# Two warm-up matmuls fewer, and two transposed copies exchanged between ScalarE and VectorE, in the opening of a linear-attention and SwiGLU kernel

## The chip, the cores and the metric

One core of a Trainium2 chip. The metric is the device time of one execution in microseconds (us). Executions of one kernel differ by some tenths of a microsecond, so medians are given with their spread. A profile is one execution. Its span runs about 1.8 us shorter than the time of the execution. Engines are named as in the profile: PE (tensor engine, matmuls), ACT (ScalarE), DVE (VectorE), POOL (GpSimd), SP (SyncE, which issues loads and stores).

## The reference, cut to what matters

Inputs q, k, v are 8 batches x 8 heads x 576 tokens x 64, in float32. Attention without a score matrix comes first, a gated feed-forward block after it.

```python
q_s = softmax(q, over the 64 features)
k_s = softmax(k, over the 576 tokens)
kv  = einsum('bhsd,bhse->bhde', k_s, v)        # one 64x64 matrix per head
x   = einsum('bhsd,bhde->bhse', q_s, kv)       # then to tokens x 512
g   = x @ w_gate
out = (g * sigmoid(g) * (x @ w_val)) @ w_out   # 512 -> 1536 -> 512
```

## The kernel before: the parts that matter

Heads are worked in two groups of four per batch (G = 0, 1). The opening is batch 0's attention, written out by hand: it has to end before the first gate matmul. `BANKS` splits the nine token blocks into five and four, one PSUM bank each. `spin(n)` issues n matmuls on zeros, only to keep PE busy.

```python
for G in range(NG):                       # loads of batch 0, on SyncE
    load("q", q, 0, G); kd.append(load("k", k, 0, G))
d = nc.gpsimd.dma_start(out=v16[0], ...)  # values, cast on the way, after the first keys
for t0, t1 in BANKS:                      # values of group 1, in two pieces
    nc.gpsimd.dma_start(out=v16[1][:, :, 64*t0:64*t1], ...)
... # then the weights w_gate / w_val in slices, then w_out in four slices (w_dma), on GpSimd

spin(8)
spin(6, first)                # the first of them waits for the first row sum
key_sum(0)                    # column sums of exp(k): 9 small matmuls, reciprocal on DVE
turn_pe(0, 0, 0); turn_pe(0, 0, 1)        # PE transposes of the normalised queries
turn_out(0, 0, 0, nc.scalar)              # copy out of PSUM
exp_of("k", 0, 1)
turn_out(0, 0, 1, nc.scalar)
norm_mul(0, 1, BANKS)         # DVE: exp(q) times 1/rowsum, group 1
spin(6)
kv_first(0)                   # first K^T V, 36 matmuls of 64x64
key_sum(1)
scale_first(0, nc.scalar)     # K^T V scaled into kn
turn_pe(0, 1, 0); turn_pe(0, 1, 1)
turn_out(0, 1, 0, nc.vector); turn_out(0, 1, 1, nc.vector)
xp0 = x_mm(0, 0, 0), x_mm(0, 0, 1)
kv_first(1, *BANKS[0]); kv_first(1, *BANKS[1])
... # copies of x, second scaling, x of group 1, copies of x

after = w_dma[0]              # batch 1's loads wait for the first slice of w_out
for what, src in (("q", q), ("v", v), ("k", k)):
    ...load(what, src, 1, G, ..., after=after)
for m in range(MT):           # gate and value matmuls of batch 0's 576 tokens
    m_unit(0, S, m, by_group=(m == 0))
exp_of("q", 1, 0); exp_of("q", 1, 1)      # behind the last silu on ACT
norm_sum(1, 0); norm_mul(1, 0); norm_sum(1, 1)
... # output matmuls of batch 0, between them batch 1's attention:
i = norm_mul(1, 1)
...
turn_pe(1, 1, 0); turn_pe(1, 1, 1)        # the transposes at 46 us
... # then K^T V and x of batch 1, then seven chunks of the feed-forward block
```

The softmax here doesn't subtract the row's maximum and nothing guards it: scores larger than these inputs give would overflow.

Of the kernel before, what the change touches and what calls it, by code (L numbers as in the profile page):

```python
# [15 lines left out]
def kernel(  # L16
# [10 lines left out]
    nc = tc.nc  # L27
# [19 lines left out]
    def bank(name):  # L47
        return psp.tile([128, 512], FP32, tag="ps", name=name)
# [57 lines left out]
    def copy(eng, out, in_):  # L106
        if eng is nc.scalar:
            nc.scalar.copy(out=out, in_=in_)  # L108
        else:
            eng.tensor_copy(out=out, in_=in_)  # L110
# [5 lines left out]
    def exp_of(what, b, G, pieces=((0, T),)):  # L116
        s = st.setdefault((b, G), {})
        e = s["e" + what] = at.tile([128, T, 2, 64], BF16, tag="e" + what, name="e" + what)
        src = raw[what, b, G].rearrange("p h (t d) -> p t h d", d=64)
        for t0, t1 in pieces:  # L120
            nc.scalar.activation(out=e[:, t0:t1], in_=src[:, t0:t1], func=AF.Exp)  # L121
# [21 lines left out]
    def norm_mul(b, G, pieces=((0, T),), engs=None):  # L143
        s = st[b, G]
        eq2 = s["eq"].rearrange("p t h d -> p (t h) d")
        qs = s["qs"] = at.tile([128, T, 128], BF16, tag="qs", name="qs")
        for (t0, t1), eng in zip(pieces, engs or (nc.vector, nc.vector)):
            n = 2 * (t1 - t0)
            last = eng.tensor_mul(  # L149
                qs[:, t0:t1, :].rearrange("p t (h d) -> p (t h) d", d=64),  # L150
                eq2[:, 2 * t0:2 * t1, :],
                s["rr"][:, 2 * t0:2 * t1].to_broadcast([128, n, 64]),
            )
        return last

    def turn_pe(b, G, i):
        s = st[b, G]
        if i == 0:
            s["qt"] = at.tile([128, T, 128], BF16, tag="qt", name="qt")
        t0, t1 = BANKS[i]  # L160
        tp = s["tp", i] = psp.tile([128, 1024], BF16, tag="ps", name="tp")
        for t in range(t0, t1):
            j = t - t0
            nc.tensor.transpose(  # L164
                out=tp[:, j * 128:(j + 1) * 128], in_=s["qs"][:, t, :], identity=ident
            )

    def turn_out(b, G, i, eng):
        s = st[b, G]
        t0, t1 = BANKS[i]  # L170
        copy(
            eng,
            s["qt"][:, t0:t1, :],
            s["tp", i][:, 0:(t1 - t0) * 128].rearrange("p (t c) -> p t c", c=128),
        )
# [19 lines left out]
    def x_mm(b, G, i):  # L195
        s = st[b, G]
        t0, t1 = BANKS[i]
        xp = [bank("xp") for _ in range(2)]
        for g in range(2):
            for h in range(2):  # L200
                r = slice(64 * h, 64 * h + 64)
                nc.tensor.matmul(  # L202
                    out=xp[h][64 * g:64 * g + 64, 0:64 * (t1 - t0)],
                    lhsT=s["kn"][r, g, :],
                    rhs=s["qt"][r, t0:t1, 64 * g:64 * g + 64],
                    start=True, stop=True,
                )
        return xp

    def x_out(b, G, i, xp, engs=(nc.scalar, nc.vector)):  # L210
        t0, t1 = BANKS[i]
        n = 64 * (t1 - t0)
        c0 = b * S + 64 * t0
        for h in (h for h in range(2) if engs[h] is not None):
            copy(engs[h], xt[:, 2 * G + h, c0:c0 + n], xp[h][:, 0:n])
# [137 lines left out]
    with tc.manual_schedule():  # L353
# [31 lines left out]
        def spin(n, after=None):  # L385
            idle = bank("idle")
            for _ in range(n):
                i = nc.tensor.matmul(out=idle, lhsT=zero[:, 0:128], rhs=zero, start=True, stop=True)  # L388
                if after is not None:
                    tc.add_manual_dep(i.ins, after.ins.name, SYNC, reason="start of the warm-up")  # L390
                    after = None
# [12 lines left out]
        def kv_first(G, t0=0, t1=T):  # L404
            s = st[0, G]
            if t0 == 0:
                s["kv"] = [bank("kv") for _ in range(2)]
            for t in range(t0, t1):
                for g in range(2):
                    for h in range(2):  # L410
                        nc.tensor.matmul(  # L411
                            out=s["kv"][g][HALF[h], 0:64], lhsT=s["ek"][HALF[g], t, h, :],
                            rhs=v16[G][HALF[g], h, 64 * t:64 * t + 64],
                            start=(t == 0), stop=(t == T - 1),
                        )

        def scale_first(G, eng1):
            s = st[0, G]
            kn = s["kn"] = at.tile([128, 2, 64], BF16, tag="kn1", name="kn1")
            nc.scalar.mul(kn[:, 0, :], s["kv"][0][:, 0:64], s["kvr"][:, 0:1])  # L420
            if eng1 is nc.scalar:
                nc.scalar.mul(kn[:, 1, :], s["kv"][1][:, 0:64], s["kvr"][:, 1:2])
            else:
                nc.vector.tensor_scalar_mul(kn[:, 1, :], s["kv"][1][:, 0:64], s["kvr"][:, 1:2])
# [5 lines left out]
        turn_pe(0, 0, 1)  # L430
        turn_out(0, 0, 0, nc.scalar)
        exp_of("k", 0, 1)
        turn_out(0, 0, 1, nc.scalar)
        norm_mul(0, 1, BANKS)
        spin(6)
        kv_first(0)
        key_sum(1)
        scale_first(0, nc.scalar)
        turn_pe(0, 1, 0)
        turn_pe(0, 1, 1)  # L440
        turn_out(0, 1, 0, nc.vector)
        turn_out(0, 1, 1, nc.vector)
        xp0 = x_mm(0, 0, 0), x_mm(0, 0, 1)
        kv_first(1, *BANKS[0])
        kv_first(1, *BANKS[1])
        x_out(0, 0, 0, xp0[0], (nc.scalar, None))
        scale_first(1, nc.vector)
        x_out(0, 0, 0, xp0[0], (None, nc.vector))
        x_out(0, 0, 1, xp0[1])
        xp1 = x_mm(0, 1, 0), x_mm(0, 1, 1)  # L450
        x_out(0, 1, 0, xp1[0])
# [153 lines left out]
```

## Time and profile before

| | |
|---|---|
| time, three runs known at the start | 311.29, 311.95, 312.0 us |
| span of the profiled execution | 309.7 us |
| first gate matmul (end of the opening) | 14.22 us |
| end of the last silu of batch 0 on ACT | 37.58 us |
| first gate matmul of the next chunk | 51.13 us |

Two rows of the slices of the page are worth a look. Each digit is the busy share of 1/40 of the span in tenths, about 7.7 us. PEclk is the granted clock, DMA the busy share of the 16 DMA engines.

```profile
PEclk9999999999999999999999999999999999999999
DMA  7999999999347815590739352605310302020133
```

The DMA engines are busy 90% or more (a 9) from the second to the tenth slice, to 77 us. The clock row reads 9 from the start, although the first warm-up matmuls run at half speed (0.427 us apart, later 0.216): the row knows of no record before the clock's first change, at 10.17 us. Starts of single matmuls tell more here than that row does.

### The profile page before, as it was taken

How to read it: one execution, taken by the hardware profiler on the slowest of the kernel's cores; microseconds unless marked ns; L12 is line 12 of the kernel's file. 1: busy time of each engine (PE TensorE's matmuls, PEld its weight loads, DVE VectorE, ACT ScalarE, POOL GpSimd, SP SyncE). 2: the span in 40 equal slices, each digit the busy share in tenths (PEclk: the TensorE clock that was granted, in tenths of full speed). 3: DMA queues.
4: the chain of work that ended last, by engine and by line, in shares of the span. 5: the costliest groups of instructions: out<-in, count | busy, mean ns of one | idle time of the engine just before them, and what ended most of it. 6: DMA issues, size and time to landing. Idle time of an engine off the chain costs nothing.

```text
span 309.7 us, 5467 instructions
## 1 busy us (share of the span) xinstructions
PE 302.8 (98%) x2182; PEld 150.3 (49%) x2182; DVE 161.9 (52%) x286; ACT 146.3 (47%) x214; POOL 32.8 (11%) x39
## 2 busy tenths in 40 slices
PE   6999999999999999999999999999999999999995
PEld 2688745554445444454445444544444444444443
DVE  3844477945754566365826492639353324433421
ACT  5843578785674375547464737455043113312300
POOL 2960021510200110002000200000000000000000
PEclk9999999999999999999999999999999999999999
DMA  7999999999347815590739352605310302020133
GB/s 273 189 195 207 275 389 389 349 219 389 79 87 200 327 33 114 135 382 13 144 74 353 102 121 61 186 0 107 72 35 0 70 11 56 3 68 8 26 71 103
DMA packets 43018, 45.78 MB, mean 148 GB/s; under 512 B 19568, under 2 KB 28272, under 8 KB 42992
## 3 DMA queue, kind: packets, MB, share of 16 engines
q1 hardware_dynamic: 34096, 39.95, 43.4%
q0 software_dynamic: 8752, 5.31, 12.0%
q8 instruction: 17, 0.28, 0.4%
q10 hardware_dynamic: 144, 0.16, 0.2%
q14 instruction: 9, 0.07, 0.1%
HBM read 37.75 MB, written 9.44 MB: 152 GB/s over the span
## 4 chain that ended last, share of the span: by engine, by line
PE 96%; DMA 1%; DVE 0%; ACT 0%; issue 0%
PE g_ps L284 30%; PE u_ps L284 30%; PE o_ps L317 29%; PE kv L189 2%; PE xp L245 1%; PE idle L388 1%; DMA q<-in_q_dram 1%; PE tp L164 1%; PE o_ps L338 1%; DVE rs L135 0%; PE xp L202 0%; PE kv L411 0%; ACT eq L121 0%; ACT xt L259 0%; PE ks L397 0%; DVE o_sb L342 0%
## 5 line engine op out<-in xcount | busy, mean ns | idle before, releaser
L291 ACT ACTIVATE sg<-g_ps 128x512 bf16<-128x512 f32 (+2 forms) x120 | 64.7, 554 | 133.6 <-PE g_ps L284 120.5
L293 DVE TENSOR_TENSOR hr<-sg,u_ps 128x512 bf16<-128x512 bf16 (+3 forms) x120 | 72.5, 616 | 86.3 <-PE u_ps L284 80.7
L284 PE MATMUL g_ps<-xt,wg 128*128 128x512 bf16 (+2 forms) x480 | 111.4, 358 | 0.1
L284 PE MATMUL u_ps<-xt,wv 128*128 128x512 bf16 (+2 forms) x480 | 111.3, 358 | 0.0
L317 PE MATMUL o_ps<-wo,hr 128*128 128x512 bf16 x420 | 93.9, 379 | 0.0
L284 PEld LDWEIGHTS <-wv 128*128 128x128 bf16 x480 | 46.9, 98 | 46.4
L284 PEld LDWEIGHTS <-wg 128*128 128x128 bf16 x480 | 46.3, 98 | 45.5 <-issue 0.6
L317 PEld LDWEIGHTS <-hr 128*128 128x128 bf16 x420 | 40.9, 98 | 48.6
L110 DVE COPY o_sb<-o_ps 128x512 f32<-128x512 f32 x33 | 22.4, 680 | 39.0 <-PE o_ps L317 39.0
L124 POOL CAST vb<-v 128x1152 bf16<-128x1152 f32 x14 | 17.8, 1277 | 135.8 <-DMA v<-in_v_dram 106.6
L135 DVE TENSOR_REDUCE rs<-eq 128x18 f32<-128x1152 bf16 (+2 forms) x18 | 21.7, 1213 | 12.7 <-ACT eq L121 12.7
L149 DVE TENSOR_TENSOR qs<-eq,rr 128x1152 bf16<-128x1152 bf16 (+2 forms) x18 | 22.1, 1234 | 0.1
L121 ACT ACTIVATE eq<-q 128x1152 bf16<-128x1152 f32 (+2 forms) x18 | 18.3, 1051 | 4.1 <-DMA q<-in_q_dram 4.0
L121 ACT ACTIVATE ek<-k 128x1152 bf16<-128x1152 f32 (+2 forms) x17 | 17.9, 1101 | 0.5 <-DMA k<-in_k_dram 0.5
L291 ACT ACT_TABLE_LOAD x12 | 15.4, 1283 | 0.2
L121 ACT ACT_TABLE_LOAD x11 | 14.1, 1283 | 0.2
L388 PE MATMUL idle<-zero 128*128 128x512 bf16 x20 | 7.9, 560 | 2.6 <-DVE rs L135 1.4
L259 ACT CAST xt<-xp 128x512 bf16<-128x512 f32 x14 | 7.8, 586 | 4.5 <-PE xp L245 4.5
L260 DVE CAST xt<-xp 128x512 bf16<-128x512 f32 x14 | 9.0, 683 | 0.7 <-PE xp L245 0.7
L189 PEld LDWEIGHTS <-ek 64*64 64x64 bf16 x504 | 6.3, 107 | 1.7 <-ACT qt L108 0.4
L189 PE MATMUL kv<-vb,ek 64*64 64x65 bf16 x504 | 6.7, 194 | 0.0
L245 PE MATMUL xp<-qt,kn 64*64 64x512 bf16 (+1 forms) x112 | 6.7, 292 | 0.0
(44 smaller groups left out, 67.4 us busy)
## 6 DMA issues: line engine op xcount, KB each, us to landing
q<-in_q_dram SPq DMA_DIRECT2D x16, 576.0 KB, 5.4
out_dram<-o_sb SPq DMA_DIRECT2D x70, 128.0 KB, 2.3
k<-in_k_dram SPq DMA_DIRECT2D x12, 576.0 KB, 7.2
v<-in_v_dram SPq DMA_DIRECT2D x12, 576.0 KB, 9.1
wo<-in_moe_w_out_dram POOLq DMA_DIRECT2D x4, 384.0 KB, 15.4
k<-in_k_dram SPq DMA_DIRECT2D x4, 320.0 KB, 8.2
k<-in_k_dram SPq DMA_DIRECT2D x4, 256.0 KB, 8.1
v<-in_v_dram SPq DMA_DIRECT2D x2, 320.0 KB, 6.9
```

Source lines behind the costliest of these rows:

```text
L110: eng.tensor_copy(out=out, in_=in_)
L121: nc.scalar.activation(out=e[:, t0:t1], in_=src[:, t0:t1], func=AF.Exp)
L124: return nc.gpsimd.tensor_copy(out=vbs[G][:, :, :, 0:64], in_=raw["v", b, G].rearrange("p h (t d) -> p t h d", d=64),)
L135: i = nc.vector.reduce_sum(out=rs[:, 2 * t0:2 * t1], in_=eq2[:, 2 * t0:2 * t1, :], axis=mybir.AxisListType.X)
L149: last = eng.tensor_mul(qs[:, t0:t1, :].rearrange("p t (h d) -> p (t h) d", d=64), eq2[:, 2 * t0:2 * t1, :], s["rr"][:, 2 * t0:2 * t1].to_ ...
L189: nc.tensor.matmul(out=kv[g][HALF[h], c:c + 65], lhsT=ek[HALF[g], t, h, :], rhs=vbs[G][HALF[g], t, h, :], start=(t == 0), stop=(t == T - 1),)
L245: nc.tensor.matmul(out=o[h][HALF[g], c:c + 64 * (t1 - t0)], lhsT=kn[HALF[h], g, G, :], rhs=qt[G][HALF[h], t0:t1, 64 * g:64 * g + 64], star ...
L284: nc.tensor.matmul(out=gu[a][i][:, 0:w_], lhsT=(wg, wv)[a][:, kk, ms], rhs=xt[:, kk, c:c + w_], start=(kk == 0), stop=(kk == KT - 1),)
L291: nc.scalar.activation(out=sg[:, 0:w_], in_=g_ps[:, 0:w_], func=AF.Silu)
L293: nc.vector.tensor_mul(hr[:, m, r:r + w1], sg[:, 0:w1], u_ps[:, 0:w1])
L317: nc.tensor.matmul(out=o_ps, lhsT=hr[:, m, r0:r0 + 128], rhs=wo[:, m, :], start=(m == 0), stop=(m == MT - 1),)
L388: i = nc.tensor.matmul(out=idle, lhsT=zero[:, 0:128], rhs=zero, start=True, stop=True)
```

## The change

Its intent: PE reaches the first K^T V sooner, with four warm-up matmuls ahead of it instead of six. ACT is relieved of a copy where it is wanted for scaling, and DVE makes that copy in a time when it had nothing to do. In exchange ACT takes one of the later copies. The last hunk also puts DVE's copy of x before its half of the second scaling, where it had come after it.

```diff
         exp_of("k", 0, 1)
-        turn_out(0, 0, 1, nc.scalar)
         norm_mul(0, 1, BANKS)
-        spin(6)
+        turn_out(0, 0, 1, nc.vector)
+        spin(4)
         kv_first(0)
@@ (key sum, scaling and transposes as before)
-        turn_out(0, 1, 0, nc.vector)
+        turn_out(0, 1, 0, nc.scalar)
         turn_out(0, 1, 1, nc.vector)
@@ (x and the second K^T V as before)
-        x_out(0, 0, 0, xp0[0], (nc.scalar, None))
+        x_out(0, 0, 0, xp0[0])
         scale_first(1, nc.vector)
-        x_out(0, 0, 0, xp0[0], (None, nc.vector))
```

## The prediction

Passages that no trace of this case shows are cut from the text below, and the cuts are marked: statements about the clock, about changes between matmul sizes and about the DMA engines, and, with the clock rival, how a late turn of the clock would come about and what time it would give; that was the author's estimate and was not shown. The forecast's own sum goes from 0.43 us off PE (step 1) over 0.29 (step 2) and 0.13 (step 5) to a gain of 0 at the end (step 7), and the time is taken from runs, 311.8 us in a range of 311.1 to 312.5.

> **What bounds the kernel now.** I read the page first, then the chain that ended last inside the opening, then the waits of the tensor engine (PE), then the landings of the loads, and last the starts of single PE instructions over the whole run, looking for gaps.
>
> The page's first line says that PE is the bound on average:
>
> ```profile
> PE 302.8 (98%) x2182; PEld 150.3 (49%) x2182; DVE 161.9 (52%) x286; ACT 146.3 (47%) x214; POOL 32.8 (11%) x39
> ```
>
> The change lies between 10 and 15 us, so the next view is the chain there (start, length in us, what):
>
> ```profile
> 10.17 1.35 PE idle L388 x6
> 11.53 0.41 PE kv L411 x36
> 11.94 0.31 PE ks L397 x9
> 12.25 0.52 PE tp L164 x9
> 12.77 0.37 PE xp L202 x8
> 13.14 0.36 PE kv L411 x35
> ...
> 13.52 0.30 DVE kn L424
> ...
> 13.84 0.45 PE xp L202 x8
> 14.29 0.60 PE g_ps L284 x4
> ```
>
> The reader is to see that the warm-up matmuls (L388) stand in this chain as if they were work, and that PE's one real stop in the opening is the wait for `kn` of the second head group before 13.84 (0.42 us in the list of waits). From 14.29 on it is gate and value matmuls without a gap.
>
> Two other engines and a load run beside it, and their ends are floors for PE. The exponential of the second key group on ScalarE (ACT) and the query normalisation on VectorE (DVE), from the timeline:
>
> ```profile
> 10.37 1.17 ACT L121 ACTIVATE ek<-k 128x1152 bf16<-128x1152 f32 x1
> ...
> 10.45 1.43 DVE L149 TENSOR_TENSOR qs<-eq,rr 128x640 bf16<-128x640 bf16 x2
> ```
>
> And the last piece of the second group's values, issued at 7.91 us, whose row says 5.0 us to landing (12.95 us in the trace):
>
> ```profile
> L361 POOL DMA_DIRECT2D v<-in_v_dram x1: 733/733/733, 7.9 to 7.9; - x1
> ...
> DMA to landing us min/median/max: 5.0/5.0/5.0
> ```
>
> Now the view that decides the prediction, much later: batch 1. Its first query load is issued at 31.82, after a weight transfer, and needs 7.1 us, so it lands at 38.94. From there ACT, then DVE:
>
> ```profile
> 38.96 1.16 ACT L121 ACTIVATE eq<-q 128x1152 bf16<-128x1152 f32 x1
> ```
> ```profile
> 40.16 1.35 DVE L135 TENSOR_REDUCE rs<-eq 128x18 f32<-128x1152 bf16 x1 [1.42 <-ACT eq L121]
> 41.54 0.27 DVE L140 RECIPROCAL rr<-rs 128x18 f32<-128x18 f32 x1
> 41.84 1.36 DVE L149 TENSOR_TENSOR qs<-eq,rr 128x1152 bf16<-128x1152 bf16 x1
> 43.12 1.35 DVE L135 TENSOR_REDUCE rs<-eq 128x18 f32<-128x1152 bf16 x1
> 44.50 0.27 DVE L140 RECIPROCAL rr<-rs 128x18 f32<-128x18 f32 x1
> 44.80 1.36 DVE L149 TENSOR_TENSOR qs<-eq,rr 128x1152 bf16<-128x1152 bf16 x1
> ```
>
> and PE at the same place:
>
> ```profile
> 44.30 1.89 PE L317 MATMUL o_ps<-wo,hr 128*128 128x512 bf16 x8
> 46.22 0.40 PE L164 MATMUL tp<-ident,qs 128*128 128x128 bf16 x4
> ```
>
> DVE is busy without a gap from 40.16 to 46.16, and PE's transposes of the second query group start at 46.22, the moment the last `qs` is written. The eight output matmuls before them start 0.216 us apart, so PE had streamed them by 44.30 + 8 x 0.216 = 46.03. It waits 0.19 us there, too short to show in the list of waits, because the drawn end of a matmul covers it. This place hangs on a load, not on when PE came.
>
> [...] warm-up matmuls start 0.427 us apart until 9.97 and 0.216 us apart from 10.29, and the granted clock turns full at 10.17. [...] the two removed ones are warm. [...] the trace shows 0.09 us at each passage between 128x128 and 64x64 matmuls (11.15 + 0.216 to 11.46), and the change removes none. [...] The DMA row is 9 or more in nearly every slice from 2 to 40 us[...].
>
> **The change part by part.**
>
> 1. *Two warm-up matmuls fewer.* 2 x 0.216 = 0.43 us off PE: the first K^T V can start at 11.03 instead of 11.46. Its values landed at 10.72, so nothing holds it.
> 2. *What holds PE next.* That K^T V takes 0.41 us to the next group, so the key sum of group 1 could start at 11.44, but ACT ends its `ek` only at 11.54, and nothing moved that. With the 0.04 us from a writer's end to PE's start seen elsewhere it starts at 11.58 instead of 11.87. Of 0.43 us, 0.29 is left.
> 3. *Transposes and first x.* Unchanged 0.83 us from key sum to the first x matmul: 12.41 instead of 12.70. The second bank of queries is normalised at 11.88; its transposes come at 12.10. No wait.
> 4. *The copies exchanged.* ACT loses a 512-column `qt` copy (0.58 us, of which 0.11 is overlap) and gains the 640-column one (0.69 us); DVE the reverse (0.49 and 0.41 us). In favour: ACT is free when the first K^T V ends, so it scales `kn` by 12.07, before PE asks at 12.41; DVE copies group 0's second bank at 11.80 to 12.21, in a time when it sat idle (0.41 us before 12.28). Against: ACT now copies 12.29 to 12.98, then an x copy to 13.30, which is near 13.34, where its `kn` scaling is wanted. It just fits.
> 5. *Second K^T V.* It starts at 12.68 instead of 12.97, but its last 16 matmuls need the value piece that lands at 12.95: start 13.00, 0.13 us of stream, out at 13.30 instead of 13.43. The gain falls to 0.13 us.
> 6. *Scaling and last x.* DVE needs 0.09 + 0.28 us, so `kn` is ready at 13.67, x starts at 13.71 (was 13.84) and the first gate matmul at 14.09 (was 14.22). Its weights land at 13.68; the value weights at 14.45 against a need of 14.59. The later slices land before their use also when that comes 0.13 us sooner.
> 7. *The sum at the end.* PE reaches the place at 46.2 us earlier by 0.13 us and waits there 0.32 instead of 0.19 us, for a chain that began with a landing at 38.94. The gain at the end is 0. After 51.2 us PE's only gaps are the 0.09 us drains, so nothing gives anything back or takes more.
>
> **The rivals.**
>
> *The gain lasts (-0.13 to -0.43 us, 311.5 to 311.8).* For it: the chain of waits names only PE from 14 to 310 us. Against it: the 0.19 us gap at 46.22, and the full DVE chain behind it. It would need the query load of batch 1 to land sooner too.
>
> *The value load or ACT becomes the bound and the opening is later.* If ACT's longer order (640-column copy, x copy, `kn`) slips by 0.1 to 0.2 us, x starts at 13.84 or later, so the opening gains nothing. The time is again the old one, since the 0.19 us at 46.22 takes a loss only beyond what PE is early.
>
> *The clock stays cold longer.* Fewer warm-up matmuls leave PE about 0.2 us of idle before the key sum. [...] Against it: the turn at 10.17 stands before the first removed instruction, and the three runs before lie within 0.7 us.
>
> **Range and chances.** The mechanism gives 0 at the end; half of the rival that the gain lasts is worth 0.1 us. From the median of 311.95 and the profiled run's 311.57 I take 311.8. The three runs spread 311.29 to 312.0, so the range is that spread and some of another day's: 311.1 to 312.5. A change of 2% would be 6.2 us; the whole opening up to the first gate matmul is 14 us, and the instructions touched sum to under 3 us. Either verdict but "same" needs something that no view shows: 0.01 each.
>
> **What would show it right or wrong.** Right: four L388 matmuls after 9.97; the key sum at about 11.58, behind ACT's `ek`; the second K^T V split by the landing near 12.95; x at 13.6 to 13.75; first gate matmul near 14.1; DVE's block of 40.16 to 46.16 unmoved; transposes still at 46.2, and everything after on the old times. Wrong: the transposes at 46.2 move with the opening, or the query load lands at another time; or PE's clock turns late; or the ACT order makes the last x later than 13.84. A shift of the landing near 38.94 by some tenths moves the end by as much in either kernel, and would hide the effect.

## The result, and the profile after

The changed kernel took 311.45 us (median of 6 runs, 311.14 to 312.51), the kernel before 311.51 us in the 6 runs then known (311.29 to 312.0). The ratio is 1.0, with a 95% interval of 0.9984 to 1.0017. No difference can be told. The interval is about half a microsecond to either side, so no time taken here could have told the prediction (0) from its first rival (0.13 to 0.43 us less): what decides between them has to come from profiles.

The profiled opening is not what was predicted. This is the chain that ended last in it (start, length in us, what):

```profile
1.75 6.69 DMA q<-in_q_dram
...
8.46 0.75 ACT eq L121
...
9.23 1.43 DVE rs L135 x2
...
10.68 0.27 DVE rr L140
...
10.98 1.44 DVE qs L149 x2
...
12.47 0.40 PE tp L164 x4
12.87 0.37 PE xp L202 x8
13.23 0.35 PE kv L411 x36
13.59 0.30 ACT kn L420
...
13.94 0.46 PE xp L202 x8
14.40 0.60 PE g_ps L284 x4
```

No warm-up matmul is left in it. It now begins with the load of the second queries and runs over ACT's exponential and DVE's normalisation of them, and the first gate matmul starts at 14.34 us, 0.12 *later* than in the profile of before. The PE timeline shows what became of the two matmuls (start, length, instruction, and in brackets the idle time before it and what ended it):

```profile
8.94 1.03 PE L388 MATMUL idle<-zero 128*128 128x512 bf16 x4
11.25 0.32 PE L411 MATMUL kv<-v,ek 64*64 64x64 bf16 x17 [1.28 <-DMA v<-in_v_dram]
```

In this execution the clock had turned full at 5.41 us, not at 10.17, so the matmuls on zeros from 6.36 on came 0.216 us apart, and all of them were over by 9.97. PE then stood for 1.28 us until the first values landed at 11.21, where they had landed at 10.72 before. Two more warm-up matmuls, 0.43 us, would have fitted into that stop nearly three times.

At 46 us, the place that carried the prediction, ACT and PE read:

```profile
37.83 1.28 ACT L121 ACT_TABLE_LOAD   x1
39.12 1.16 ACT L121 ACTIVATE eq<-q 128x1152 bf16<-128x1152 f32 x1
```
```profile
44.53 1.89 PE L317 MATMUL o_ps<-wo,hr 128*128 128x512 bf16 x8
46.37 0.34 PE L164 MATMUL tp<-ident,qs 128*128 128x128 bf16 x3
```

The transposes moved from 46.22 to 46.37, with the opening, which the prediction had named as a sign that it is wrong. The exponential starts right behind the activation table's load, without an idle time in brackets; the queries had landed at 38.55. So here ACT was not waiting for the load at all.

Two profiles of two kernels thus differ by their loads and by when the clock turned full at least as much as by the change. The experiments had to part these.

### The profile page after: what moved, and what is told of

The parts are those of the page before. It is cut to its first block, busy times and chain, and to the rows that moved or that the text cites. A ratio compares the mean times of both kernels' runs of the same rounds, so it can differ in the third digit from the quotient of the medians.

```text
span 309.9 us, 5438 instructions
## 1 busy us (share of the span) xinstructions
PE 299.8 (97%) x2155; PEld 149.5 (48%) x2180; DVE 161.5 (52%) x286; ACT 146.4 (47%) x214; POOL 32.9 (11%) x39
## 4 chain that ended last, share of the span: by engine, by line
PE 94%; DMA 2%; DVE 1%; issue 1%; ACT 1%; SPq 0%
PE g_ps L284 30%; PE u_ps L284 30%; PE o_ps L317 29%; DMA q<-in_q_dram 2%; PE kv L189 2%; PE xp L245 1%; PE o_ps L338 1%; PE tp L164 0%; DVE qs L149 0%; DVE rs L135 0%; SPq L77 0%; PE xp L202 0%; ACT eq L121 0%; ACT xt L259 0%; DVE o_sb L342 0%
## 5 line engine op out<-in xcount | busy, mean ns | idle before, releaser
L317 PE MATMUL o_ps<-wo,hr 128*128 128x512 bf16 x403 | 92.5, 379 | 0.9 <-issue 0.2
L135 DVE TENSOR_REDUCE rs<-eq 128x18 f32<-128x1152 bf16 (+2 forms) x18 | 21.7, 1214 | 13.2 <-ACT eq L121 13.2
L388 PE MATMUL idle<-zero 128*128 128x512 bf16 x18 | 6.1, 491 | 2.8 <-DVE rs L135 1.5
```

Source lines behind the costliest of these rows:

```text
L135: i = nc.vector.reduce_sum(out=rs[:, 2 * t0:2 * t1], in_=eq2[:, 2 * t0:2 * t1, :], axis=mybir.AxisListType.X)
L317: nc.tensor.matmul(out=o_ps, lhsT=hr[:, m, r0:r0 + 128], rhs=wo[:, m, :], start=(m == 0), stop=(m == MT - 1),)
```

## The experiments

Theory A, formed on this result: *the opening ends when loads let it, whichever kernel it is; the warm-up matmuls mostly fill stops that a load makes anyway.* Its rivals: the change itself moved those loads (B), the opening is hidden at the end whatever it does (B2), the warm-up matmuls are on the path (C), the exchanged copies cost something that hides a gain (D), the clock needs the warm-ups (E). And, from the prediction, that the place at 46 us takes up what the opening gains or loses.

All twelve runs gave correct results. spin_only is an edit of the kernel before, the ten others after it are edits of the changed kernel. The ratios of all of them are against the kernel before; the changed kernel itself was not run again.

**The kernel before, looked at again**, unedited.

> The kernel before, unchanged, for a second look at its opening. Theory A (loads and the clock's phase differ from execution to execution, and set the opening more than the change does): the landings of the first values (10.72 us before, 11.21 after), of the second queries (7.92 and 8.44) and the turn of the clock (10.17 and 5.41) come out on still other values, so the first gate matmul lies between 14.0 and 14.6 in no fixed relation to which kernel it is. Rival B (the change itself moved these landings): they repeat the values before to 0.1 us, and the gate matmul is at 14.2.

One run, 311.39 us (its state is unknown, as it is a single one). First values at 11.07, second queries at 8.25, clock at 9.80, first gate at 14.12. The same program thus has landings 0.35 us apart in two executions, and rival B is not needed for the loads. One profile is little, and it did not show the clock turning early, as after did (5.41). But that turn, and the issue of these loads (at 1.75 and 6.3 to 6.5 us), come before the first instruction that the change touches (9.97 in before), and late4 below, with four warm-up matmuls, turned at 9.51.

**Each half of the change alone.**

```diff
 # spin_only: the kernel before with
-        spin(6)
+        spin(4)
 # copies_only: the changed kernel with
-        spin(4)
+        spin(6)
```

> The two warm-up matmuls less, the copies as before. Theory A: the time is that of before within 0.2% (311.2 to 311.9), because what is saved (0.43 us at the warm clock) is taken up first by the landing of the first values, at the latest by the load-fed chain at 46.2 us. Rival C (the warm-up matmuls are on the path to the end): 311.1, 0.4 us less than before.

> The copies exchanged, six warm-up matmuls kept. Theory A: the time is that of before within 0.2%; in the profile VectorE's copy of group 0's second bank lies directly behind its normalisation. Rival D (the exchange costs ScalarE time on the path, and hides a gain of the fewer warm-ups): 0.2 to 0.4 us slower than before, with the last scaling of ScalarE more than 0.1 us behind the arrival of the second K^T V.

Two warm-up matmuls fewer alone: 311.35 us (6 runs, 311.28 to 312.1), ratio 0.9995, interval 0.9981 to 1.001. The copies alone: 311.71 us (6 runs, 311.46 to 313.24), ratio 1.0012, interval 0.9992 to 1.0033. The kernel before: 311.5 us (11 runs, 311.19 to 312.64). Neither half can be told from nothing. But the times alone do not exclude the rivals either: the 0.4 us that C expected to gain and the 0.2 to 0.4 us that D expected to lose lie inside these intervals. The profiles have to speak. In that of the copies alone, ACT's and DVE's halves of the second scaling end at 13.70 and 13.74, where they ended at 13.79 and 13.80 before: ACT is not late, and nothing in it speaks for D. In that of spin_only the values' landing held the first K^T V, as expected (PE waited 0.8 us for it). But the loads came early there, and the opening ended 0.46 us sooner than in before; 0.35 us of that was then lost to a late weight slice, which nobody had expected (step 6 below).

**Many more, and hardly any.**

```diff
 # spin20
-        spin(4)
+        spin(20)
 # spin1
-        spin(4)
+        spin(1)
```

> The changed kernel with 20 in place of 4 warm-up matmuls before the first K^T V: 16 x 0.216 = 3.46 us more of them. Theory A: the opening is late by 3.46 less what PE idled there (between 0.2 us with a late clock and 1.5 us with an early one), and past the load at 38.9 us, so the end is late too: 313.4 to 314.8 us. Rival B2 (the opening is hidden at the end whatever it does): 311.5.

> The changed kernel with 1 warm-up matmul in place of 4 before the first K^T V (one is kept so that the PSUM banks rotate as they did). Theory A (the first values' landing, near 10.6 to 11.2 us, holds the first K^T V once the warm-up matmuls end before it): no time is gained over 4, 311.2 to 311.8, and the first K^T V starts within 0.05 us of that landing. Rival C (warm-up matmuls are on the path): 3 x 0.216 = 0.65 us less, 310.8. Rival E (too few for the clock): 312 or more, with the clock turning after 10.3.

With 20: 313.76 us (4 runs, 313.33 to 314.31), ratio 1.007 (1.0051 to 1.0089). The PE timeline:

```profile
8.89 4.48 PE L388 MATMUL idle<-zero 128*128 128x512 bf16 x20
13.30 0.48 PE L411 MATMUL kv<-v,ek 64*64 64x64 bf16 x36
```

The values had landed at 10.73; from there on the matmuls on zeros only delay the first K^T V. The first gate came at 16.08, 1.74 us behind that of after, and the span was 311.50 instead of 309.87 us, 1.63 longer: rival B2 falls, the opening is not hidden at the end. With 1: 311.65 us (6 runs, 311.33 to 313.77), ratio 1.0007 (0.9977 to 1.0037). The first K^T V started at 11.01, 0.04 us behind its values (10.96). Nothing gained over four, and no run near the 310.8 of C (the fastest took 311.33); C falls for numbers this small. The one run of 313.77 us has no profile, but the record lists its granted clock: 0.989, the lowest of all runs here. The kernel before had a run of 313.74, with 0.998, so long runs have other causes too. An estimate from the clock: 0.011 x 312 = 3.4 us lost, or 6.8 us at half speed. Part of such a loss can lie at the end, when PE is done (in after the last matmul ended at 306.11 us and the granted clock was 0.50 from 309.20 to the end), but so much was seen in no other run. So rival E may have come true in one of six executions with a single matmul; this stays open.

**What the opening waits for.** The ten profiles of the opening with its loads in the usual order and the usual warm-up ahead, in us. "L388" is the number of warm-up matmuls right before the first K^T V, "values 0" are those of head group 0, "queries 1" those of group 1, "qs" is the end of DVE's normalisation of group 1's queries, "piece 2" the landing of the last values of group 1.

| profile | L388 | clock full | values 0 land | first K^T V | queries 1 land | qs | piece 2 | first gate |
|---|---|---|---|---|---|---|---|---|
| before | 6 | 10.17 | 10.72 | 11.46 | 7.92 | 11.88 | 12.95 | 14.22 |
| before_again | 6 | 9.80 | 11.07 | 11.27 | 8.25 | 12.21 | 12.94 | 14.12 |
| copies_only | 6 | 9.71 | 11.09 | 11.22 | 8.27 | 12.23 | 12.56 | 14.16 |
| after | 4 | 5.41 | 11.21 | 11.25 | 8.44 | 12.41 | 12.93 | 14.34 |
| spin_only | 4 | 4.95 | 10.64 | 10.68 | 7.63 | 11.70 | 12.62 | 13.76 |
| late4 (below) | 4 | 9.51 | 11.15 | 11.19 | 8.37 | 12.33 | 12.65 | 14.25 |
| closed (below) | 4 | 3.88 | 10.85 | 10.90 | 8.03 | 12.00 | 13.43 | 14.57 |
| last4 (below) | 4 | 4.85 | 11.15 | 11.20 | 8.32 | 12.28 | 13.26 | 14.40 |
| spin1 | 1 | 9.29 | 10.96 | 11.01 | 8.02 | 11.99 | 13.21 | 14.36 |
| spin20 | 20 | 5.12 | 10.73 | 13.30 | 7.92 | 11.88 | 12.73 | 16.08 |

Three things can be read from it. First, with four or one the first K^T V starts 0.04 to 0.05 us behind the landing of its values, in every row. Second, qs ends 3.96 or 3.97 us behind the landing of its queries (4.07 in spin_only). Third, the first gate matmul is, to 0.02 us, the later of qs + 1.92 and piece 2 + 1.15, in eight of the ten rows: 12.41 + 1.92 = 14.33 for after, 13.43 + 1.15 = 14.58 for closed. The two sizes 1.92 and 1.15 are read from these same rows, so this is a description and not yet a test. The two exceptions are spin20 and *before*, whose 14.22 lies above both (13.80 and 14.10). The profile that the prediction was built on is the one of three with six matmuls where the warm-up set the end of the opening, because its clock turned last and its queries came first. In the other two the saving would have been nothing, by this reading.

The rows also show how far an opening with its loads in this order moved: the second queries landed between 7.63 and 8.44 us, the first values between 10.64 and 11.21, the last values between 12.56 and 13.43. The clock turned full between 3.88 and 5.41 us in five rows and between 9.29 and 10.17 in the other five, all with the same fourteen matmuls on zeros at the start. Why there are two groups is not shown.

**The second queries late.** The table suggests that these queries hold the opening; this run tests it by moving them. No run moved piece 2 alone, so its share stays a reading of the table.

```diff
-        for G in range(NG):
-            load("q", q, 0, G)
-            kd.append(load("k", k, 0, G))
+        load("q", q, 0, 0)
+        kd.append(load("k", k, 0, 0))
+        kd.append(load("k", k, 0, 1))
+        load("q", q, 0, 1)
```

> The changed kernel with the second query load of batch 0 put behind the second key load, so that it lands near 9.4 to 9.9 us instead of 7.6 to 8.4. Theory A2 (after six profiles: the first gate matmul comes 5.9 us after that landing, through ScalarE's exponential, VectorE's sum, reciprocal and multiply and PE's transposes, when no warm-up holds it): first gate at 15.3 to 15.8 us, and the time 1.0 to 1.6 us longer, 312.5 to 313.2. Rival (the values' landing or the warm-up matmuls hold the opening): first gate at 14.2 to 14.6, time 311.5.

The queries landed at 9.60, qs ended at 13.57, the first gate came at 15.57 (13.57 + 1.92 = 15.49): as expected of A2. ACT takes the exponentials in the program's order, so that of the second keys was late with the queries (it ended at 12.52, and PE waited 1.07 us for it); the multiply still came last, PE waited 0.15 us for it before 13.62. The time was not as expected: 314.42 us (4 runs, 312.74 to 314.69), ratio 1.0078 (1.0052 to 1.0105), more than the opening accounts for. The stretches of the profile show the rest (start:end, length; busy time of PE, PEld, DVE, ACT, POOL with counts; granted clock; DMA share and GB/s):

```profile
8.50:12.00 3.50, 1.74 (x44) 1.00 (x44) 1.64 (x4) 2.38 (x4) 3.50 (x6) 1.00 1.23 177
12.00:15.40 3.40, 2.20 (x70) 1.56 (x70) 3.31 (x10) 2.62 (x7) 3.40 (x6) 1.00 1.79 177
15.40:18.80 3.40, 3.40 (x22) 2.06 (x15) 0.84 (x3) 2.54 (x5) 3.40 (x5) 0.50 1.54 191
18.80:22.00 3.20, 3.20 (x28) 2.56 (x27) 1.60 (x4) 0.97 (x3) 1.82 (x3) 1.00 1.33 203
```

The clock fell back to half from 15.38 to 18.79 us, and batch 0's gate and value matmuls took 24.98 us from the first one's start to the last one's instead of 23.42. That is 1.56 us on top of the 1.2 that the opening was late. Why it fell is not shown. The longest stop of PE in the 6.9 us before was 1.15 us. PE was busy only 2.20 of the 3.40 us before; but in the stretch before that it was busy even less, 1.74 of 3.50 us, and the clock stayed full. So the drawn busy time of such a stretch does not by itself tell when it falls. One of the four runs took 312.74 us, inside the range expected, and its mean granted clock is 1.0; the other three have 0.994, which is about what 3.41 us at half speed make of 312 us. No profile of that run was kept, and the kernel before has runs at 0.994 with ordinary times (311.45, 311.69), so this remains an inference.

**Almost no warm-up at all**, three matmuls on zeros in the whole opening instead of eighteen.

```diff
-        spin(8)
-        spin(6, first)
+        spin(1)
+        spin(1, first)
@@
-        spin(4)
+        spin(1)
```

> The changed kernel with 3 warm-up matmuls in all instead of 18, for the rival of the clock. If the clock needs them, it is still cold when the gate matmuls start[...]: the opening is about 1.5 us later (its PE work at half speed)[...]. If the clock turned early anyway, 311.5.

313.75 us (4 runs, 313.15 to 314.2), ratio 1.0056 (1.0023 to 1.009). The clock turned at 18.55, after the first gate matmuls, as expected of E. The time is a little below the range that was given; that range rested on how long the clock stays at half speed, which no trace had shown by then. A caution on reading: the stretches of this profile give

```profile
8.00:15.10 7.10, 5.08 (x116) 3.83 (x116) 5.70 (x14) 5.11 (x10) 7.10 (x11) 1.00 1.44 175
15.10:18.50 3.40, 3.40 (x21) 1.96 (x14) 0.82 (x2) 2.40 (x4) 3.29 (x5) 1.00 1.61 191
18.50:22.00 3.50, 3.50 (x30) 2.78 (x29) 1.64 (x4) 1.17 (x5) 2.05 (x3) 1.00 1.35 202
```

with a clock of 1.00 throughout, but 21 matmuls in 3.4 us and then 30 in 3.5: up to 18.55 there was no record yet, and PE ran at half speed. So the warm-up is worth some 2 us (313.75 against 311.53 us of the kernel before). The edit took twelve of the fourteen matmuls at the start and three of the last four; spin1 took the same three and kept its time in five of six runs, so rival E holds for those at the start. No run shows a use of the fifth and sixth.

**The load at 46 us, later.** The prediction said that this place hangs on the landing of batch 1's queries. If so, a later landing must cost time, and must swallow a late opening.

```diff
-        after = w_dma[0]
+        after = w_dma[2]      # late4, and late20 with spin(20)
+        after = w_dma[3]      # last4, and last20 with spin(20)
```

> The changed kernel, batch 1's query load held back until the third instead of the first slice of the output weights is there (35.6 instead of 31.8 us). Theory A (the place at 46 us goes by the later of this landing and of PE's own chain): the load lands near 41 to 42.7, the transposes follow 7.28 us later at 48.3 to 50, and the end is 2 to 4 us late: 313.5 to 315.5. Rival (the load does not matter there): 311.5.

> The same late load with 20 instead of 4 warm-up matmuls. Theory A: the 16 more cost nothing beyond late4, within 0.5 us, where they cost 2.3 us with the early load, since ScalarE is ready for the queries at 40.75, before the load lands. Rival (delays of the opening and of the load add up): 2.3 us more than late4.

This first pair missed its aim. In late4 the third slice landed 3.8 us behind the first (35.18 and 31.39), but the load then needed less time, 3.7 and 4.1 us instead of 6.8 to 7.1 (why is not shown; a clause on it in the expectation of last4 is cut), and landed at 38.91 in late4 and 39.36 in late20, hardly later than in other executions (38.41 to 39.17). late4 took 312.46 us (4 runs, 312.25 to 312.96), ratio 1.0024 (0.9996 to 1.0052), so its loss is not clear of noise; in its profile the second queries of batch 1 (42.03 instead of 40.3 to 41.2) and the keys (46.53 instead of 45.0 to 45.7) were late. late20 took 314.06 us (4 runs, 313.36 to 314.38), ratio 1.007 (1.0041 to 1.0099). The 16 matmuls cost 1.6 us between the medians, where 2.3 was the cost with the early load and 0.5 at most was expected: ACT was ready at 40.70 in late20, after the landing, so there was no late load to hide behind. What late20 lost at 46 us, 0.68 us, lies in a multiply of DVE, beside which a cast of POOL ran:

```profile
43.29 1.14 POOL L124 CAST vb<-v 128x1152 bf16<-128x1152 f32 x1 [21.70 <-DMA v<-in_v_dram]
```
```profile
43.60 2.04 DVE L149 TENSOR_TENSOR qs<-eq,rr 128x1152 bf16<-128x1152 bf16 x1
```

POOL's cast of batch 1's values started 0.3 us before DVE's multiply, and the multiply took 2.04 us instead of 1.36, which is these 0.68 us. In the kernel before the order is the other way round, DVE starting at 41.84 and POOL at 42.20, and there the multiply took 1.36 us and the cast 2.01, where the median of that kernel's 14 casts is 1.15:

```profile
42.20 2.01 POOL L124 CAST vb<-v 128x1152 bf16<-128x1152 f32 x1 [20.27 <-DMA v<-in_v_dram]
```

In after the order is the same as in before (DVE at 42.00, 1.36 us; POOL at 42.52, 1.85 us). So in these three profiles the one that started second took longer, DVE by 0.68 us, POOL by 0.86 and 0.70. That the two hold each other up is inferred from this; no run parts them. The order turned where the values landed at 43.23 instead of 42.15 us and DVE's multiply came 1.8 us later.

> The load of batch 1's queries held back until the last weight slice (near 39.7 us), with 4 warm-up matmuls: holding it to the third slice moved the landing by no more than 0.4 us[...]. Theory A: it lands at 42 to 43, the first gate of the next chunk moves from 51.2 to 54 to 55.5, and the time is 314.5 to 316. Rival (the load does not matter): 311.5.

> The same with 20 warm-up matmuls, which with the early load cost 2.3 us. Theory A: nothing beyond last4 within 0.5 us, as ScalarE is ready for the queries at 40.75, before they land at 42 to 43. Rival (the delays add): 2.3 us more than last4.

The second pair, behind the last weight slice: last4 took 314.86 us (4 runs, 314.05 to 315.8), ratio 1.0109 (1.0087 to 1.013); last20 took 314.83 us (4 runs, 314.0 to 315.29), ratio 1.0104 (1.0085 to 1.0123). Held late enough, the load costs 3.3 us, and the 16 matmuls that cost 2.3 us with the early load then cost nothing that can be told, with intervals of 0.6 to 0.7 us to either side of each. Late load and late opening do not add; the later one counts. In last4 the queries landed at 42.09:

```profile
42.12 1.16 ACT L121 ACTIVATE eq<-q 128x1152 bf16<-128x1152 f32 x1 [2.49 <-DMA q<-in_q_dram]
```
```profile
46.42 0.68 PE L164 MATMUL tp<-ident,qs 128*128 128x128 bf16 x9 [1.70 <-DVE qs L149]
```

(these are the transposes of the first query group, which wait for the same chain). In last20's profile the two ran nearly level: the queries landed at 41.13 and ACT was done with its table at 41.80, so from batch 0's last value matmul to the next gate it took the usual 13.41 us (the table in step 7 below):

```profile
40.52 1.28 ACT L121 ACT_TABLE_LOAD   x1
41.81 1.16 ACT L121 ACTIVATE eq<-q 128x1152 bf16<-128x1152 f32 x1
```

**The two gaps after the opening.** If the opening is worth nothing, the gaps that every profile shows at 46 and 51 us may be worth more.

```diff
-        i = norm_mul(1, 1)
+        i = norm_mul(1, 1, BANKS)
@@
-        turn_out(1, 1, 0, nc.scalar)
+        turn_out(1, 1, 0, nc.vector)
@@
-        o_mm(3, p3, m0=6, m1=11)
+        o_mm(3, p3, m0=6, m1=10)
         x_and_next_kv(1, with_kv=False)
-        o_mm(3, p3, m0=11)
+        o_mm(3, p3, m0=10)
```

> The changed kernel with the two PE gaps that every profile shows after the opening narrowed: batch 1's last normalisation in two pieces (gap of 0.12 us and more before the transposes at 46 us), one transposed copy given to VectorE, and one more output matmul left for the gap of 0.25 us before the gate matmuls at 51 us. Theory A: from the end of batch 0's last value matmul to the first gate of the next chunk 13.40 us becomes 13.15 to 13.25, whatever the opening did; 0.2 us of 311 is below what timing resolves (311.0 to 311.6). Rival: another wait (the keys' landing, ScalarE) takes its place and 13.4 stays.

311.82 us (6 runs, 310.86 to 312.09), ratio 1.0004 (0.9989 to 1.002). The gap at 46 us is gone, that at 51 us shrank from 0.255 to 0.150, but the way from batch 0's last value matmul to the next gate took 13.67 us and not 13.2. The list of PE's waits has a new line:

```profile
PE kv L189 <- ACT ek L121: 0.2, 1, 0.2
```

In this execution batch 1's first keys landed at 46.76, in the others of the usual order between 45.0 and 45.7. Whether the edit is worth its 0.2 us when they come on time is open; it does not beat the kernel before measurably, and its three parts were not run apart.

## Why the prediction was right or wrong, point by point

The time is right: 311.8 predicted, 311.45 measured, no change as said. But any change of a few tenths would have read the same, so that is little proof, and the account of it is right only in parts. Both its main reasons fail: that nothing but the warm-up holds the first K^T V (step 1), and that a load at 46 us swallows the gain (step 7).

*Step 1, the two matmuls.* "The first K^T V can start at 11.03 instead of 11.46. Its values landed at 10.72, so nothing holds it": this is the step that failed first. It took a landing of one execution as a property of the kernel. The values landed between 10.64 and 11.21 in the ten profiles, and in each one with four matmuls or fewer this landing held the first K^T V. The 0.43 us were there to be saved in the profile of before, with its clock turning at 10.17 and its values at 10.72; in before_again and copies_only the first K^T V came only 0.20 and 0.13 us behind its values, of which 0.04 is the usual lag, and qs held the first gate anyway.

*Steps 2 and 3, what holds PE next.* Predicted was the key exponential at 11.54, with no wait of the transposes. In the profile after, the exponential ended at 11.36 and held nothing; the transposes waited 0.29 us for DVE's qs, 3.97 us behind queries that landed at 8.44 instead of 7.92. The run with those queries moved (q_last) showed that the first gate follows them.

*Step 4, the copies.* Right. ACT's half of the scaling ended at 13.89 and DVE's at 13.92: it "just fits". The step left out that DVE now copies x before its scaling (13.24 to 13.72 in after). That did no harm: DVE ended 0.03 us behind ACT, where it was 0.02 before.

*Step 5, the last values.* The mechanism is right, and so is the way from the landing to the first gate (12.95 to 14.09, 1.14 us predicted; 1.15 in the table). Whether it comes last depends on the execution: it held the opening in spin_only, spin1, closed and last4, and not in after.

*Step 6, the first gate at 14.09.* It came at 14.34, and the value weights, at 14.90 instead of 14.45, held the first value matmul 0.11 us. The step's sentence that the weights come in time is of the same kind as step 1. In spin_only the opening was 0.46 us ahead of before, and batch 0's matmuls then took 23.77 us instead of 23.42, since a slice of w_val landed only at 16.94 (15.90 before).

*Step 7, the place at 46 us.* "This place hangs on a load, not on when PE came" is wrong for most executions, and 0 came out of it for a poor reason. The line that the prediction needed stands in the answer of which it quotes the next one:

```profile
37.59 1.28 ACT L121 ACT_TABLE_LOAD   x1
```

ACT was loading its table until 38.88, 0.06 us before the queries landed, and it starts that behind the last silu, so behind PE. From the start of batch 0's last value matmul to the start of the next chunk's first gate it takes (in us)

| profile | ACT's table loaded | queries of batch 1 landed | last value matmul to next gate |
|---|---|---|---|
| before_again | 38.78 | 38.57 | 13.41 |
| after | 39.11 | 38.55 | 13.41 |
| spin_only | 38.76 | 38.71 | 13.41 |
| copies_only | 38.81 | 38.41 | 13.41 |
| spin20 | 40.74 | 38.51 | 13.41 |
| before | 38.88 | 38.94 | 13.48 |
| spin1 | 39.01 | 39.17 | 13.58 |
| last4 | 39.63 | 42.09 | 16.20 |

Where the queries are there before ACT has its table, the stretch is 13.41 us to the hundredth and moves with PE (in last20, q_last and no_warm too, whatever their opening; late4, late20 and closed are longer, as told above). Of the gap at 46 us 0.12 us belongs to that: last silu, table load, exponential and 6 us of DVE are a little longer than PE's own work. Only in before and spin1 of the ordinary executions did the load come last, by 0.06 and 0.16 us, and only that much could be absorbed. The pair with the load held back to the last slice shows the mechanism itself is real.

*After that.* "After 51.2 us PE's only gaps are the 0.09 us drains": right as to the gaps, which lie between 128x128 and 64x64 matmuls; that PE drains in them is not shown. From that gate to the end it takes 258.56 to 258.63 us in all profiles but late4 and last4 (258.92 and 259.37), where later loads were late too.

Put together, an ordinary execution ends at first gate + 23.42 + 13.41 + 258.6 us: 14.12 + 295.43 = 309.55 for before_again, whose span was 309.56. What the opening loses reaches the end (spin20). What it wins reaches the end only where the weights keep up, as far as one profile shows: spin_only's opening was 0.46 us ahead of before, and 0.35 of it went to the late slice of w_val, so the sum gives 309.19 and the span was 309.51. But in most executions there was little to win: loads set the end of the opening, and fewer warm-up matmuls do not shorten it.

*The rivals.* "The gain lasts" was weighed against the wrong thing: not the place at 46 us but the loads of the opening and of w_val take the gain, and no run here could show a gain of 0.13 us. The clock rival was rightly given little for this change, since the turn at 10.17 came before the first matmul that was removed, and q_last and no_warm showed what it costs when it does happen: about 1.5 us in batch 0's matmuls, 24.98 and 24.94 us instead of 23.42.

## What to carry to other kernels

A chain read from one execution puts a filler matmul and a real dependence side by side; ask of each landing in it whether a second profile of the same kernel has it at the same time, before counting a saving against it in tenths of a microsecond. Filler that ended before a load landed was free here, and taking it away gained nothing; what that may cost is the clock (no_warm, 313.75 us, and perhaps one run of spin1), so look at the granted clock of every run, not of the profiled one alone. Read the line above the one that supports you: here it was the table load. A wait on two chains that end nearly together is a maximum: whether a gain passes it depends on which of them was last in that execution.
